# The spectrum tasks of a convolution wait until the last block of powers has been issued

## The chip, the cores and the metric

The kernel runs on one core of a Trainium2 chip. The metric is the device time of one execution in microseconds (us), taken as the median over several runs.

## The reference

The output puts two independent layers side by side, each for a sequence of 2048 rows and a width of 448.

```python
# A: a state-space convolution
dt = exp(log_dt);  A = -exp(log_A_real) + 1j*A_imag;  C = (C_real + 1j*C_imag)*dt[:, None]
P = exp((A*dt[:, None])[:, :, None] * pos)          # 448 channels x 256 states x 2048 positions
K = 2*einsum("dn,dnl->dl", C, P).real                # one filter of 2048 taps for each channel
y = irfft(rfft(u_t, 2*L) * rfft(K, 2*L))[:, :, :L]   # causal convolution
a = y.T + u*D_skip
# B: softmax attention, 16 heads of 28
q, k, v = split(x @ wqkv);  p = softmax(q @ k.T * 28**-0.5);  b = (p @ v) @ wo
out = concatenate([a, b], -1)
```

## The kernel before

An opening stage projects queries, keys and values and prepares seeds of the powers for A. Everything after it is one long loop, and this case lies in the loop. The attention is cut into 16 units (4 groups of 4 heads, 4 chunks of 512 queries), and each unit into 16 tiles of 128 keys. The loop runs over `NS` = 256 steps `s`, with `u, kt = divmod(s, 16)`: step 192 begins unit 12. In each step TensorE multiplies four score tiles (`s0` to `s3`, written to `pss`), ScalarE takes their exponentials (`p`), and TensorE multiplies those of the step before with the values (`pv`, written to `po`). Up to step 236 each step also takes row maxima for a unit further ahead (`m0` to `m3`, scores in `pm`, reduced on VectorE to `mx`); the steps from 237 on are called `late` and have none.

The work of layer A is laid into the gaps. The order inside a step is written out by hand, and from here on every engine executes its instructions in the order in which they are issued:

```python
ORDER = ('m0', 's0', 'm1', 's1', 'v', 'f', 'pv', 'f', 'v', 'k', 'm2', 's2', 'm3', 's3', 'v')
```

- `k`: the filters. There are `NB` = 56 blocks. `k_begin(s)` starts block b in step 3.5 b or later, once the lists of the block before are empty. It fills `powers["e"]` with 9 GpSimd operations (three doublings; the last one has tiles of 128x1024) and `powers["g"]` with 9 parts on VectorE. Each `k` issues 3 of the first list and each `v` one of the second. Three products of the block follow as tasks 4, 5 and 6 steps after its start: two read both sets of powers (`pm<-e,g`), the third is `pm<-w,ko`.
- `f`: a slot, `slot(s)`. Late steps have one more. A slot takes the first thing that is due: an urgent task, a projection of a finished unit (`p_due`), a product of a block (`m_due`), and otherwise a task that `f_slot` picks, first of kind "s", then of kind "f".
- Kind "s" are the spectra: 16 jobs (2 halves of the channels by 8), possible from step 192 on, loaded two steps (`FL`) ahead. One job is four tasks: `forth(0)`; `last`, which is `forth(1)` and the two joins; `back(0)`, at least `GAP` = 3 slots behind `last`; `back(1)`. A `forth` is 16 small matmuls (`pm<-yk,mw`) and two products with the input's spectrum on VectorE (`pr<-pm,ub`). A join is two complex sums on GpSimd (`p<-pr,pr`). A `back` is 16 matmuls (`pm<-p,mw`), a copy on ScalarE and a store `z<-y` on SyncE's queue.
- Kind "f" are 8 finishing jobs of four tasks `one(i)` (`pm<-zi,wb`, then VectorE `ot<-pm,ut`). They read `z` back (`zi<-z`), three steps (`FL`) ahead; the first half of them needs 8 finished spectra, the second half all 16. `skip` multiplies their input on GpSimd (`ut<-ut,dsk`).

`fin(u)` ends a unit: in the second step after its end, `sums` and `scale` use VectorE (`rb`, `pm<-r`, `on`), and for the last four units four projections follow (`project`, 32 matmuls on `ua`). After the loop the remaining tasks are drained slot by slot.

Of the kernel before, what the change touches and what calls it, by code (L numbers as in the profile page):

```python
# [92 lines left out]
def body(ctx, tc, a, out):  # L93
# [5 lines left out]
    def pool(stack, name, bufs=1, space=None, side=None):  # L99
        kw = {} if space is None else {"space": space}  # L100
        if side:
            kw["side"] = side
        return stack.enter_context(tc.tile_pool(name=name, bufs=bufs, reuse_waits="tile", **kw))
# [807 lines left out]
    def job(j, p, uh_p, ps, b0=(2, 1, 1, 2, 2), b1=(2, 2)):  # L911
        kind, f, i = j
        return spectrum(f, i, p, uh_p, ps, b0) if kind == "s" else finish(f, i, p, ps, b1)
# [11 lines left out]
    powers = {"g": collections.deque(), "e": collections.deque()}  # L925
# [20 lines left out]
    k_due = collections.deque(range(NB))  # L946
# [14 lines left out]
    def f_load(s_, kind):  # L961

        if not f_jobs[kind] or f_loaded[kind]:
            return
        _, f, i = f_jobs[kind][0]
        if kind == "f" and s_done[0] < (f + 1) * N1 // 4:
            return
        if (kind, f, i) == ("f", 0, 0):
            if f_ready["s", 1] == NS:
                return  # L970
            f_p["f", 0] = f_p["f", 1] = pool(f1_st, "ff_p")
        if (kind, f) not in f_p or f_ready.get((kind, f), 0) > s_ + 2:
            return
        load, tasks, ahead = job(f_jobs[kind].popleft(), f_p[kind, f], kq_p, w_tile)
        load()
        if ahead:
            f_ahead.append((s_ + FL[kind] - 1, ahead))
        f_loaded[kind].append((max(f_ready.get((kind, f), 0), s_ + FL[kind]), tasks))

    def f_slot(s_, kind):  # L980
        f_load(s_, kind)
        while f_ahead and f_ahead[0][0] <= s_:
            f_ahead.popleft()[1]()
        if not f_tasks[kind]:
            if not f_loaded[kind] or f_loaded[kind][0][0] > s_:
                return False
            f_tasks[kind].extend(f_loaded[kind].popleft()[1])
            f_load(s_, kind)
        gap, t = f_tasks[kind][0]
        if n_slot[0] < f_next[kind] + gap:  # L990
            return False
        f_tasks[kind].popleft()
        t()
        s_done[0] += kind == "s" and not f_tasks[kind]
        f_next[kind] = n_slot[0]
        f_load(s_, kind)
        return True
# [10 lines left out]
    def slot(s_):  # L1008
        n_slot[0] += 1
        while free and free[0][0] <= n_slot[0]:  # L1010
            free.popleft()[1]()
        if urgent and urgent[0][0] <= n_slot[0]:
            urgent.popleft()[2]()
        elif s_ >= NS and f_slot(s_, "s"):
            pass
        elif p_due and p_due[0][0] <= s_:
            p_due.popleft()[1]()
        elif m_due and m_due[0][0] <= s_:
            m_due.popleft()[1]()
        elif u_due and u_due[0][0] <= s_:  # L1020
            u_part(*u_due.popleft()[1:])
        else:
            f_slot(s_, "s") or f_slot(s_, "f")
# [158 lines left out]
```

## Time and profile before

| | |
|---|---|
| runs | 1278.78, 1279.68 and 1281.36 us, median 1279.68 us |
| profiled execution | 1280.71 us, its span 1278.9 us |
| busy in the span: TensorE, VectorE, ScalarE, GpSimd | 94%, 74%, 75%, 66% |
| mean granted TensorE clock | 0.982 |

Times in the trace are us from the start of the span. A row of the timeline has the start, the duration, the engine, the line of the code, the operation, the written tile, an arrow, the read tiles, the shape and how many instructions the row merges; in brackets stands how long the engine had been idle and what ended that. All instructions are issued by one helper, so that all rows have its line, and tiles are told apart by their names. A row of the table by stretches has the stretch, its length, the busy time of TensorE, its weight loads, VectorE, ScalarE and GpSimd (with instruction counts), the granted TensorE clock, the share of the DMA engines and GB/s. A step is found in the trace by its first maximum matmul, `pm<-kdif,qhat`.

### The profile page before, as it was taken

The numbers are of one execution on the slowest core, as the hardware profiler recorded it, in microseconds if no ns is written. First come the engines' busy times: TensorE is split into PE (matmuls) and PEld (weight loads), VectorE is DVE, ScalarE is ACT, GpSimd is POOL, SyncE is SP. The second block draws the span as 40 slices with busy tenths as digits, with TensorE's granted clock in tenths as the row PEclk, the third lists the DMA queues.
The fourth block names the chain that finished last, engine by engine and source line by source line (L and its number), as shares of the span: only waits on it lengthen the run. The fifth ranks groups of instructions, "written<-read, shape, count | busy, mean of one in ns | idle before, by whom it ended". The sixth has DMA issues, their size and how long they took to land.

```text
span 1278.9 us, 31211 instructions
## 1 busy us (share of the span) xinstructions
PE 1199.8 (94%) x11569; PEld 669.9 (52%) x11569; DVE 942.6 (74%) x2138; ACT 959.2 (75%) x2146; POOL 843.5 (66%) x728
## 2 busy tenths in 40 slices
PE   6778887999999999999999999999997999999998
PEld 4667664555555555555555555555553545545333
DVE  5788966878777878887789889888996665646312
ACT  5888865788888888888888888888885766756553
POOL 2666740897788888778599999889984222424321
PEclk8999899899999999999999999999998999999999
DMA  6678789437554545365533133422314443647666
GB/s 195 215 254 297 268 287 358 120 88 195 155 147 115 164 118 178 110 228 178 170 88 104 49 88 103 148 82 71 99 43 141 157 161 135 210 151 236 201 179 164
DMA packets 203377, 206.08 MB, mean 161 GB/s; under 512 B 98201, under 2 KB 162265, under 8 KB 201177
## 3 DMA queue, kind: packets, MB, share of 16 engines
q1 hardware_dynamic: 202696, 203.50, 51.6%
q8 instruction: 91, 1.49, 0.5%
q10 hardware_dynamic: 528, 0.59, 0.2%
q14 instruction: 62, 0.50, 0.1%
HBM read 121.59 MB, written 82.18 MB: 159 GB/s over the span
## 4 chain that ended last, share of the span: by engine, by line
PE 72%; DVE 13%; POOL 5%; ACT 4%; issue 3%; DMA 2%; ACTq 0%; SPq 0%; POOLq 0%; DVEq 0%
PE pm L77 40%; PE pss L77 15%; PE po L77 15%; DVE mx L77 2%; DVE tri L77 2%; ACT rl L77 1%; ACT p L77 1%; DVE rl L77 1%; POOL qhat L77 1%; DVE g L77 1%; DVE zg L77 1%; POOL p L77 1%; DMA xn<-in_B_x 1%; POOL e L77 1%; PE pt L77 1%
## 5 line engine op out<-in xcount | busy, mean ns | idle before, releaser
L77 ACT ACTIVATE p<-pss 128x512 f32<-128x512 f32 x1024 | 561.9, 610 | 127.6 <-PE pss L77 124.3
L77 PE MATMUL pss<-qhat,khat 128*128 128x512 f32 x1024 | 402.0, 399 | 2.0 <-ACT p L77 2.0
L77 DVE TENSOR_REDUCE mx<-pm 128x1 f32<-128x512 f32 x480 | 308.2, 683 | 102.1 <-PE pm L77 100.5
L77 PE MATMUL pm<-khat,qhat 128*128 128x512 f32 x749 | 327.0, 440 | 14.3 <-DVE mx L77 5.4
L77 POOL TENSOR_TENSOR e<-e,sdb 128x256 f32<-128x256 f32 x168 | 201.9, 1202 | 110.8 <-ACT e L77 101.6
L77 PE MATMUL po<-p,v 128*32 128x512 f32 x2048 | 269.6, 595 | 0.0
L77 PEld LDWEIGHTS pm<-khat,qhat 128*128 128x128 f32 x749 | 140.9, 188 | 231.1 <-ACT p L77 53.7
L77 POOL TENSOR_TENSOR e<-e,eu 128x256 f32<-128x256 f32 x168 | 248.2, 1477 | 13.2
L77 DVE CUSTOM_DVE_ANT_0 rl<-pm,rl 128x512 f32<-128x512 f32 x259 | 178.1, 688 | 68.1 <-ACT rl L77 65.8
L77 PEld LDWEIGHTS pss<-qhat,khat 128*128 128x128 f32 x1024 | 190.4, 188 | 45.5 <-issue 11.4
L77 POOL TENSOR_TENSOR eu<-e,sdb 128x256 f32<-128x256 f32 x168 | 202.0, 1202 | 0.0
L77 POOL TENSOR_TENSOR p<-pr,pr 64x448 f32<-64x448 f32 x64 | 73.1, 1142 | 149.1 <-PE pm L77 108.1
L77 ACT ACTIVATE rl<-pm 128x512 f32<-128x512 f32 x259 | 156.7, 606 | 15.6 <-PE pm L77 9.4
L77 DVE TENSOR_TENSOR g<-g,zg 128x128 f32<-128x128 f32 x392 | 162.0, 413 | 3.5
L77 PE MATMUL pm<-kdif,qhat 128*128 128x512 f32 x249 | 100.0, 402 | 6.7 <-DVE xn L77 4.3
L77 PE MATMUL pm<-xh,khat 128*128 128x512 f32 x256 | 84.4, 422 | 11.9 <-DVE hl L77 5.1
L77 DVE TENSOR_TENSOR zg<-g,zg 128x128 f32<-128x128 f32 x224 | 87.9, 393 | 5.0
L77 PE MATMUL pm<-e,g 128*32 128x64 f32 x3584 | 73.7, 223 | 10.7 <-POOL e L77 8.2
L77 PEld LDWEIGHTS pm<-e,g 128*32 128x32 f32 x3584 | 56.0, 110 | 49.1 <-POOL e L77 12.5
L77 DVE TENSOR_TENSOR pr<-pm,ub 128x448 f32<-128x448 f32 x64 | 36.8, 618 | 45.8 <-PE pm L77 30.3
L77 ACT ACTIVATE y<-pm 128x448 f32<-128x448 f32 x48 | 26.6, 555 | 58.4 <-PE pm L77 32.8
L77 ACT ACTIVATE ub<-pm 128x224 f32<-128x224 f32 (+1 forms) x96 | 38.6, 448 | 40.0 <-PE pm L77 38.1
(132 smaller groups left out, 1406.1 us busy)
## 6 DMA issues: line engine op xcount, KB each, us to landing
sdb<-sd SPq DMA_DIRECT2D x55, 336.0 KB
qhat<-q SPq DMA_DIRECT2D x64, 256.0 KB
khat<-k SPq DMA_DIRECT2D x64, 256.0 KB
sd<-sg SPq DMA_DIRECT2D x8, 1456.0 KB
k<-hl SPq DMA_DIRECT2D x16, 512.0 KB
mw<-in_mw SPq DMA_DIRECT2D x16, 512.0 KB
sd<-qhat SPq DMA_DIRECT2D x8, 896.0 KB
yu_d<-ub SPq DMA_DIRECT2D x64, 112.0 KB
```

The lines of the kernel that those rows point to most:

```text
L77: i = f(*args, **kw)
```

## The change

`f_slot` still loads the next job, but takes up no task, and runs no `skip`, while a block of powers is still to begin or a list of powers still holds something. Nothing else differs.

```diff
     def f_slot(s_, kind):
         f_load(s_, kind)
+        if k_due or powers["e"] or powers["g"]:
+            return False
         while f_ahead and f_ahead[0][0] <= s_:
             f_ahead.popleft()[1]()
```

## The prediction

> **What bounds the kernel now.** I began with the page: TensorE is busy 94% of the span and carries most of the chain that ended last, so the question is where TensorE stands still.
>
> ```profile
> PE 1199.8 (94%) x11569; PEld 669.9 (52%) x11569; DVE 942.6 (74%) x2138; ACT 959.2 (75%) x2146; POOL 843.5 (66%) x728
> PE 72%; DVE 13%; POOL 5%; ACT 4%; issue 3%; DMA 2%; ACTq 0%; SPq 0%; POOLq 0%; DVEq 0%
> ```
>
> Next came TensorE's waits from 900 us to the end (who waited for what: total, times, longest). One wait stands out: 6.5 us in one piece for powers (`e`) from GpSimd.
>
> ```profile
> PE pm L77 <- POOL e L77: 6.5, 1, 6.5
> PE pm L77 <- POOL p L77: 2.1, 3, 0.8
> ```
>
> The timelines of GpSimd and TensorE show how it comes about.
>
> ```profile
> 950.88 1.91 POOL L77 TENSOR_TENSOR e<-e,sdb 128x1024 f32<-128x1024 f32 x1
> 962.12 1.31 POOL L77 TENSOR_TENSOR e<-e,eu 128x512 f32<-128x512 f32 x1
> 976.35 4.77 POOL L77 TENSOR_TENSOR p<-pr,pr 64x448 f32<-64x448 f32 x4 [12.93 <-DVE pr L77]
> 981.20 1.91 POOL L77 TENSOR_TENSOR e<-e,sdb 128x1024 f32<-128x1024 f32 x1
> 983.07 1.90 POOL L77 TENSOR_TENSOR eu<-e,sdb 128x1024 f32<-128x1024 f32 x1
> 985.05 2.32 POOL L77 TENSOR_TENSOR e<-e,eu 128x1024 f32<-128x1024 f32 x1
> ...
> 968.75 0.96 PE L77 MATMUL pm<-yk,mw 128*32 128x224 f32 x16 [0.37 <-DVE pm L77]
> 974.05 0.94 PE L77 MATMUL pm<-yk,mw 128*32 128x224 f32 x16
> 987.42 1.08 PE L77 MATMUL pm<-e,g 128*32 128x64 f32 x32 [6.46 <-POOL e L77]
> 989.98 1.63 PE L77 MATMUL pm<-p,mw 128*32 128x224 f32 x16
> ```
>
> GpSimd had finished two of the three doublings of a block at 963.43 (962.12 + 1.31). It then stood 12.93 us, because the next in its queue were four joins of the first spectrum, which need `pr` from VectorE and so the `forth` matmuls that TensorE reaches only at 968.75 and 974.05. The last doubling, three instructions that depend on nothing of this, came behind the joins and ended at 987.37 (985.05 + 2.32); TensorE had been waiting for it since 980.97 (987.42 - 6.46).
>
> This is block 55, the last one. It cannot begin before step 192.5, so it begins in 193; its first product comes four steps on, in 197, which makes the step of 987.42 step 197. The first `forth` is due two steps after the load in 192, in 194. The doublings are issued at the `k` of steps 193, 194 and 195, and `last` in the second slot of 195, which stands before that step's `k`. The order on GpSimd follows.
>
> Here are the steps around it, from one matmul `pm<-kdif,qhat` to the next (columns: stretch, length, busy times of PE, PEld, DVE, ACT, POOL, granted clock, DMA share, GB/s). They are steps 194 to 199, step 197 cut at the end of the wait.
>
> ```profile
> 965.44:971.23 5.79, 4.68 (x65) 2.37 (x64) 5.15 (x13) 3.23 (x8) 0.00 (x0) 1.00 1.04 380
> 971.23:976.36 5.13, 4.75 (x49) 2.39 (x49) 4.22 (x10) 3.29 (x7) 0.01 (x1) 1.00 0.93 305
> 976.36:979.87 3.51, 3.38 (x16) 1.58 (x17) 3.48 (x9) 2.34 (x5) 3.39 (x3) 1.00 0.05 7
> 979.87:987.42 7.55, 1.09 (x5) 0.56 (x4) 1.50 (x4) 2.36 (x5) 7.26 (x5) 0.81 0.00 0
> 987.42:992.58 5.16, 5.16 (x60) 2.70 (x61) 0.50 (x1) 0.97 (x3) 0.00 (x0) 0.61 0.00 0
> 992.58:996.84 4.26, 4.26 (x66) 2.55 (x65) 1.98 (x5) 3.22 (x8) 0.00 (x0) 1.00 0.17 58
> 996.84:1001.07 4.23, 4.23 (x50) 2.53 (x48) 2.33 (x6) 3.09 (x7) 0.00 (x0) 1.00 0.19 60
> ```
>
> Together they take 35.63 us (1001.07 - 965.44). Step 197 takes 12.71 (7.55 + 5.16), where step 198 with the same kinds of task, one product and one `back`, takes 4.26. The excess is 8.45: the wait of 6.46 and 1.99 more, because the granted clock behind the wait was 0.61. The Trainium skill (TensorE: Matmul & The Clock Gate, What's actually happening) says that an idle window of about 3.4 us halves the clock and that about as long a busy one restores it. That would be half of 3.4, 1.7 us by its figure, instead of my 1.99, and the gain forecast below would be 0.3 us smaller.
>
> **The change, part by part.** The gate opens when the last part of the last list is issued. Powers `e` are out at the `k` of step 195. Powers `g` go one at each `v`; the first falls to the `v` behind `k` in step 193, then three a step, so the ninth goes at the second `v` of step 196, behind both slots. In step 197 the first slot belongs to the product, the second is the first that can take `forth(0)`. So: `forth(0)` moves from 194 to 197, `last` from 195 to 198, `back(0)` and `back(1)` from 197 and 198 into the two slots of 200 (three slots behind `last`), and the second job's `forth(0)` from 199 to 201. Steps 194 to 199 hold five tasks of spectra before and two after.
>
> *GpSimd's queue.* Nothing now stands between the second and the last doubling. That one takes 6.13 to 6.2 us (981.20 to 987.37 above), hence ends near 969.6. TensorE asks for it in step 197. Steps 194 to 196 are rebuilt below at 5.2, 3.48 and 3.05, so step 197 starts at 977.2 and its product a little over 1 us later (980.97 - 979.87 = 1.10), at 978.3. The cover is 8.7 us, and both the wait and the slow clock go. The joins pass behind the powers: they start at the earliest when `last` has run in step 198, when GpSimd has nothing else.
>
> *The six steps.* Costs come from steps with the same content:
>
> ```profile
> 679.77:684.86 5.09, 4.03 (x49) 1.87 (x48) 5.06 (x12) 3.54 (x8) 4.93 (x4) 1.00 0.15 54
> 850.45:856.09 5.64, 4.12 (x49) 1.98 (x48) 5.50 (x15) 3.47 (x8) 5.48 (x3) 1.00 0.79 258
> 908.43:913.33 4.90, 3.99 (x34) 1.86 (x33) 4.87 (x12) 3.82 (x8) 4.67 (x6) 1.00 0.00 0
> 920.33:923.78 3.45, 3.45 (x33) 2.02 (x32) 3.13 (x8) 3.21 (x8) 3.29 (x4) 1.00 0.00 0
> 923.78:926.83 3.05, 3.05 (x18) 1.51 (x17) 2.84 (x8) 2.47 (x6) 2.89 (x3) 1.00 0.70 138
> ```
>
> The first three are steps in which a unit is scaled beside one product, which is what step 194 becomes; VectorE is full in them. The mean is 5.2. Step 195 keeps one product, 3.45; step 196 has nothing, 3.05. Steps 197 and 198 have a product and a `forth`, 4.26 as step 198 now; step 199 one product, 3.45. The sum is 5.2 + 3.45 + 3.05 + 4.26 + 4.26 + 3.45 = 23.7 us against 35.6: 11.9 us less.
>
> *What is given back.* Three tasks of spectra now lie behind step 200. Their price is TensorE's:
>
> ```profile
> 1030.04:1033.11 3.07, 3.07 (x18) 1.50 (x16) 2.60 (x6) 2.56 (x6) 2.50 (x3) 1.00 0.51 202
> 1033.11:1037.66 4.55, 4.55 (x49) 2.62 (x48) 2.00 (x5) 4.14 (x9) 2.08 (x2) 1.00 0.16 54
> 1069.13:1073.01 3.88, 3.88 (x34) 2.03 (x33) 3.78 (x8) 2.50 (x6) 0.43 (x1) 1.00 0.94 348
> ```
>
> A step with none takes 3.07, with one 3.88, with two 4.55: 0.81 for a single task, 0.74 each in a pair. Three cost 2.2 to 2.4; I take 2.4. The order of two tasks in a step and of empty steps changes between 200 and 247, which by these rows moves 0.07 a task and is inside that. The pattern of both tasks in one step, an empty step, both `back`s in the next (1030.04 and 1033.11 are its end) stands in the trace already without a wait for joins.
>
> *The late steps.* Counting both orders slot by slot, the lag is three tasks at step 200, one from about step 224 on. It puts `last` of the fifth job of the second half into step 238 instead of 237. Late steps are short, and three slots then no longer cover two joins:
>
> ```profile
> 1178.33 4.76 POOL L77 TENSOR_TENSOR p<-pr,pr 64x448 f32<-64x448 f32 x4 [0.77 <-PE pss L77]
> 1183.15 0.96 PE L77 MATMUL pm<-p,mw 128*32 128x224 f32 x16 [0.80 <-POOL p L77]
> 1191.06 0.96 PE L77 MATMUL pm<-p,mw 128*32 128x224 f32 x16 [0.56 <-POOL p L77]
> 1193.47 0.96 PE L77 MATMUL pm<-p,mw 128*32 128x224 f32 x16 [0.78 <-POOL p L77]
> ```
>
> The fifth job waits 0.80 now, the sixth, wholly in late steps, 0.56 + 0.78 = 1.34. I give the fifth the sixth's wait and a little more for it, 0.7 us in all. The bounds are none and twice the 1.34, 2.7. The last two jobs have a projection between `last` and `back`.
>
> *SyncE's queue.* The loads of the first job stay in step 192; those of the second move from 194 to 197, to before a `forth` four steps later. The last `back` goes from step 245 to the first slot of 246, and the load of the first finishing job of the second half from the second slot of 246 to the third. The finishing jobs wait three steps for their loads, so from step 248 on both orders are the same; the drain after the loop is not touched, and I cost it at nothing, covered by that wait.
>
> The sum: 11.9 - 2.4 - 0.7 = 8.8 us. From the profiled execution that is 1280.71 - 8.8 = 1271.9; it lies 1.0 above the median of the runs, so for the median 1279.68 - 8.8 = **1270.9 us**.
>
> **The rivals.**
>
> *One step late at the end.* If `z` is not back in time or the load slips one slot, all finishing jobs of the second half come a step later.
>
> ```profile
> 1245.64:1255.00 9.36, 8.80 (x70) 3.39 (x69) 1.56 (x4) 6.30 (x14) 1.34 (x2) 1.00 1.08 311
> 1229.05 0.48 SPq L77 DMA_DIRECT2D zi<-z  x1
> 1236.29 0.58 PE L77 MATMUL pm<-zi,wb 128*32 128x224 f32 x8
> ```
>
> Three such steps take 9.36, one 3.1: 1274.0 us. For it: the margin in the order is one slot. Against it: from the issue of `zi` to its first reader there are 7.2 us now.
>
> *Slower.* The same mechanism with more steps: the finishing jobs come one per three steps, so if the gate opened so late that the lag were four steps at their first load, 12.5 us would be lost at the end: 1279.7 + 3.7 = 1283.4. It decides from three steps on (9.4 against 8.8). That needs block 55 to begin three or more steps later than 193; against it stands its first product four steps behind step 193 in the order above.
>
> *VectorE holds up GpSimd.* The last doubling moves beside a VectorE that is busy 5.15 of 5.79 and 4.22 of 5.13 us. If GpSimd got only the rest, 1.55 us, it would be short by 4.6 at 976.36 and end at 981, TensorE would wait nearly 3 us, and the clock with it: about 1275. Against it: the same instruction took 1.91 us at 950.88, in ordinary steps like that of 923.78 (VectorE busy 2.84 of 3.05), and 1.91 at 981.20, when VectorE was nearly idle. The Trainium skill (SBUF — State Buffer, Who interferes with whom) describes an exclusive lock between the two for VectorE operations with two SBUF inputs or in a two-port mode; these equal durations show no such lock here.
>
> *The change does not act,* or the wait moves to the joins in step 200: then 11.9 shrinks by 8.45 or more and the result is within 0.2% of before, 1277 to 1281. Against it: the two `forth`s that GpSimd stood for are themselves moved.
>
> **How the numbers follow.** 0.2% or 2.6 us is about what a measurement of this kernel can tell from no change. The forecast has 0.66, one step late 0.14, held-up powers 0.03, a partial gain from dearer joins 0.05, no change 0.06, slower 0.06. The first four are all faster, 0.88; same 0.06; slower 0.06. For the range: step 194 at 4.90, tasks at 0.74 and no late wait give 12.2 - 2.2 = 10.0, 1269.7; like steps differ by up to 0.7 (4.90 and 5.64), and one or two of the six better by as much make the low end 1268.5. At the high end step 194 at 5.64 and late waits of 2.7 give 11.5 - 2.4 - 2.7 = 6.4, 1273.3, and one step late 1274.0; with a little of both, 1275.5.
>
> **What would show it.** In the trace after: the three 128x1024 operations of block 55 directly behind its 128x512 ones; no wait of TensorE for `e` near step 197 and a granted clock of 1.00 there; steps 194 to 199 in about 24 us; the first joins behind the last powers; waits for `p` in late steps of about 2.8 instead of 2.1 us in total; the last nine steps unchanged. The prediction is wrong if `pm<-e,g` or the first `pm<-p,mw` still waits several us, if steps 200 to 247 grow by more than 5 us, or if the drain grows.

## The result, and the profile after

The changed kernel takes 1273.45 us (median of 4 runs, 1271.97 to 1275.26) against 1280.49 us before in the same comparison: ratio 0.9948, 95% interval 0.9936 to 0.9961, 7.0 us or 0.55% faster. Forecast were 1270.9 us, 8.8 below the median then known, and a range of 1268.5 to 1275.5, in which the result lies. The profiled execution took 1275.26 us, the longest of the four, with a span of 1273.5; the profile of a second run of the same kernel, `after_again` below, has a span of 1271.2.

GpSimd's timeline after:

```profile
962.56 1.31 POOL L77 TENSOR_TENSOR e<-e,eu 128x512 f32<-128x512 f32 x1
963.95 1.91 POOL L77 TENSOR_TENSOR e<-e,sdb 128x1024 f32<-128x1024 f32 x1
965.82 1.92 POOL L77 TENSOR_TENSOR eu<-e,sdb 128x1024 f32<-128x1024 f32 x1
967.81 2.36 POOL L77 TENSOR_TENSOR e<-e,eu 128x1024 f32<-128x1024 f32 x1
986.62 4.81 POOL L77 TENSOR_TENSOR p<-pr,pr 64x448 f32<-64x448 f32 x4 [16.45 <-DVE pr L77]
```

The last doubling of block 55 follows the second one directly and ends at 970.17. TensorE begins its product at 978.19, so 8.0 us of cover are left. The joins come 16 us later, when GpSimd has nothing else to do.

TensorE's waits from 900 us on:

```profile
PE pm L77 <- POOL p L77: 3.5, 3, 2.2
PE pss L77 <- ACT p L77: 1.7, 6, 0.3
PE pm L77 <- DVE on L77: 1.4, 3, 0.6
PE pm L77 <- DMA zi<-z: 0.9, 1, 0.9
```

The wait of 6.5 us for `e` is gone. In its place there is more waiting for joins (3.5 instead of 2.1 us) and a wait of 0.9 us for the first finishing job's read-back, which was not there before.

Steps 194 to 199 after, in the columns of the prediction:

```profile
965.89:970.47 4.58, 3.82 (x50) 1.95 (x49) 4.48 (x12) 3.07 (x7) 4.21 (x2) 1.00 1.00 376
970.47:973.95 3.48, 3.48 (x34) 1.94 (x32) 3.37 (x8) 2.81 (x6) 0.00 (x0) 1.00 0.37 141
973.95:976.99 3.04, 3.04 (x18) 1.58 (x17) 2.73 (x8) 2.55 (x6) 0.00 (x0) 1.00 0.78 180
976.99:981.82 4.83, 4.59 (x65) 2.45 (x64) 3.06 (x7) 3.07 (x8) 0.00 (x0) 1.00 0.57 216
981.82:986.62 4.80, 4.55 (x64) 2.39 (x65) 3.05 (x7) 2.79 (x7) 0.00 (x1) 1.00 0.00 0
986.62:990.24 3.62, 3.62 (x32) 2.02 (x33) 2.24 (x5) 2.79 (x6) 3.43 (x3) 1.00 0.02 5
```

They take 24.35 us (990.24 - 965.89), the clock is full throughout, and the tasks lie in the slots that the prediction counted. The rest of the run is cut at the matmuls with the values (`po<-p,v`) of step 236 and at the last group of them. The stretch between these two cuts is called the late steps from here on, what follows is the drain. First come the late steps and the drain of before, then those of the first profile after, and last two rows of the second profile, steps 194 to 199 and the late steps:

```profile
1172.36:1257.82 85.46, 81.30 (x805) 32.72 (x799) 21.45 (x48) 48.04 (x93) 28.72 (x21) 1.00 0.74 217
1257.82:1278.90 21.08, 15.84 (x180) 6.69 (x174) 4.64 (x10) 3.39 (x7) 2.09 (x1) 0.98 0.35 97
```

```profile
1162.47:1252.38 89.91, 83.79 (x821) 33.70 (x815) 21.59 (x48) 49.15 (x94) 28.68 (x21) 0.98 0.74 217
1252.38:1273.50 21.12, 15.84 (x180) 6.69 (x174) 4.64 (x10) 3.40 (x7) 2.10 (x1) 0.96 0.37 100
```

```profile
964.97:989.31 24.34, 23.15 (x257) 12.33 (x256) 18.89 (x42) 17.08 (x36) 7.64 (x5) 1.00 0.46 159
1161.54:1250.12 88.58, 82.30 (x821) 33.16 (x815) 21.57 (x48) 49.11 (x94) 28.64 (x21) 1.00 0.74 221
```

| us against before | first profile | second profile |
|---|---|---|
| up to step 194, where nothing differs | +0.45 | -0.47 |
| steps 194 to 199 | -11.28 | -11.29 |
| step 200 to the `pv` of 236 | +0.94 | +0.94 |
| from there to the loop's end | +4.45 | +3.12 |
| drain | +0.04 | 0.0 |
| span | -5.4 | -7.7 |

So 11.3 us are saved in six steps and 4.1 to 5.4 are given back, about four fifths of it after step 236.

### The profile page after: what moved, and what is told of

The parts are those of the page before. It is cut to its first block, busy times and chain, and to the rows that moved or that the text cites. A ratio compares the mean times of both kernels' runs of the same rounds, so it can differ in the third digit from the quotient of the medians.

```text
span 1273.5 us, 31219 instructions
## 1 busy us (share of the span) xinstructions
PE 1199.4 (94%) x11569; PEld 670.1 (53%) x11569; DVE 943.5 (74%) x2138; ACT 959.4 (75%) x2146; POOL 844.4 (66%) x728
## 4 chain that ended last, share of the span: by engine, by line
PE 71%; DVE 14%; ACT 5%; POOL 4%; issue 4%; DMA 1%; ACTq 0%; SPq 0%; DVEq 0%; POOLq 0%
PE pm L77 40%; PE pss L77 15%; PE po L77 15%; DVE mx L77 2%; DVE tri L77 2%; ACT rl L77 2%; ACT p L77 2%; DVE rl L77 1%; DVE g L77 1%; POOL qhat L77 1%; DVE zg L77 1%; ACT tri L77 1%; DVE sg L77 1%; DVE hl L77 1%; DVE px L77 1%
```

## The experiments

Each kernel was compared with the kernel before in the same series: median 1280.78 us for the first four, 1280.20 for the last four.

**after_again**: the changed kernel unaltered.

> The changed kernel once more, as the yardstick beside the next three. Theory (the wait of 6.46 us and the slow clock behind it go; steps 194 to 199 take 24.4 instead of 35.6 us; about 4.5 us are given back in the late steps): 6 to 8 us faster than before, about 1273 us. If the profile of the first run had a chance delay in its late steps (2.16 us for p, 0.91 us for zi), these waits are absent here and it comes nearer to 1270.9.

Measured: 1273.01 us (ratio 0.9940, 0.9928 to 0.9953). The waits for `p` are again 3.5 us in total, 1.6 the longest, and that for `zi` 1.0. They are no chance delay. The totals are equal, and TensorE is busy 1.5 us longer in the late steps of the first profile with the same instructions (83.79 against 82.30). So the 1.3 us between the two are the slow clock behind the longest wait, which only the first has.

**order_only**: only the order in GpSimd's queue.

```diff
         f_tasks[kind].popleft()
+        while kind == "s" and len(f_tasks[kind]) == 2 and powers["e"]:
+            powers["e"].popleft()()
         t()
```

> The gate is left out; only the order in GpSimd's queue is changed: what is left of the powers e is issued just ahead of the first joins. No task moves to another slot. Theory (order of GpSimd's queue): the wait for e and the slow clock go, steps 194 to 196 stay crowded, nothing lags and the late steps stay as before: 8.4 us faster, about 1272 us. Rival (the gain of the change comes from thinning out steps 194 to 196, where VectorE is full): at most 3 us faster, about 1277.5 us or more, and TensorE waits elsewhere in steps 196 to 198.

Measured: 1272.10 us (0.9931, 0.9918 to 0.9943), 8.7 us faster than before. The two stretches in its trace, steps 194 to 199 and the late steps:

```profile
963.31:990.21 26.90, 25.52 (x305) 13.98 (x304) 19.15 (x43) 18.39 (x38) 8.78 (x6) 1.00 0.47 162
1161.49:1246.94 85.45, 81.28 (x806) 32.72 (x800) 21.54 (x48) 48.16 (x93) 28.68 (x21) 1.00 0.74 219
```

On GpSimd the last doubling now ends before the joins, which still stand and wait for `pr`:

```profile
965.22 2.37 POOL L77 TENSOR_TENSOR e<-e,eu 128x1024 f32<-128x1024 f32 x1
973.97 4.81 POOL L77 TENSOR_TENSOR p<-pr,pr 64x448 f32<-64x448 f32 x4 [6.38 <-DVE pr L77]
```

With all its tasks in the slots of before, six steps shrink from 35.63 to 26.90 us, by 8.73, and the late steps stay at 85.45. GpSimd's order alone makes the whole of the wait and of the clock, and thinning out steps 194 to 196 is not needed for it: that rival falls.

**gate_last**: only the task with the joins waits, and only for the powers `e`.

```diff
         gap, t = f_tasks[kind][0]
+        if kind == "s" and len(f_tasks[kind]) == 3 and (k_due or powers["e"]):
+            return False
```

> Only the task with the joins waits, and only for the powers e: forth(0) stays in step 194, last moves from step 195 to the first slot of 196, and from step 197 on the order is that of before. Theory: steps 194 to 199 take 5.8 + 3.5 + 3.9 to 4.6 + 4.3 + 4.3 + 4.2 = 26.0 to 26.7 instead of 35.6 us, nothing is given back: 8.9 to 9.6 us faster, about 1271.3 us, 2 us faster than the whole change. Rival (the lag costs nothing, the late waits are chance): equal to the whole change within 0.7 us.

Measured: 1271.66 us (0.9929, 0.9916 to 0.9941).

```profile
964.04:990.74 26.70, 25.33 (x305) 14.16 (x304) 19.26 (x43) 18.19 (x38) 8.74 (x6) 1.00 0.47 163
1162.09:1247.53 85.44, 81.27 (x805) 32.72 (x799) 21.45 (x48) 48.05 (x93) 28.71 (x21) 1.00 0.74 217
```

Six steps take 26.70 us, the late steps 85.44 as before: nothing is given back. It comes out 1.4 us below the whole change in the medians; the intervals overlap, so that the times alone don't settle the difference, but in the traces the late steps are shorter by 3.1 us (88.58 - 85.44), and from step 194 to the end of the span it takes 304.6 us against 306.2. Its six steps are only 0.2 us better than those of `order_only`, though the second `forth` has left step 195.

**skip_with_first_task**: the whole change, `skip` issued later.

```diff
-            f_ahead.append((s_ + FL[kind] - 1, ahead))
+            tasks[0] = (0, lambda f=tasks[0][1]: (ahead(), f()))
```

> The whole change, and the GpSimd multiplication that prepares a finishing job (skip) is issued with the job's first task instead of a step earlier, so that it no longer stands ahead of the joins of step 238. Theory (part of what is given back is that joins wait behind a skip that itself waits for its transfer): TensorE's wait of 2.16 us for p in step 239 falls to about 0.7, with less of a slow clock behind it: 1.5 to 2.7 us faster than the whole change, about 1271.3 us. Rival (the joins are late because VectorE is): no difference.

Measured: 1279.27 us (0.9988, 0.9979 to 0.9997), 6 us slower than the whole change. The expectation failed, though the mechanism shows. First the changed kernel's GpSimd rows around step 238, then this kernel's of steps 235 and 236, then its waits of TensorE:

```profile
1171.32 2.11 POOL L77 TENSOR_TENSOR ut<-ut,dsk 128x896 f32<-128x896 f32 x1 [9.26 <-DVE pr L77]
1173.38 4.74 POOL L77 TENSOR_TENSOR p<-pr,pr 64x448 f32<-64x448 f32 x4
```

```profile
1158.44 4.75 POOL L77 TENSOR_TENSOR p<-pr,pr 64x448 f32<-64x448 f32 x4 [8.15 <-PE pm L77]
1163.28 2.07 POOL L77 TENSOR_TENSOR ut<-ut,dsk 128x896 f32<-128x896 f32 x1
```

```profile
PE pm L77 <- DVE ot L77: 5.1, 3, 3.4
PE pm L77 <- POOL p L77: 2.6, 4, 0.7
```

In the changed kernel a `skip` of 2.11 us stands directly ahead of the joins; without it there, the longest wait for `p` falls to 0.7 and the total to 2.6 us. But the `skip` of the finishing job before, now issued with that job's first task, stands behind the joins of step 235, `ot` waits for the `skip`, and TensorE waits for `ot`: 5.1 us, 3.37 in one piece. Behind that piece the granted clock is low, 0.59 from 1165.83 to 1170.00 us, which adds to the loss. It is the fault of the kernel before over again, with another pair of operations.

**late_joins_on_vector**: the whole change; late joins on VectorE. In the code `late[0]` holds from step 238 on; step 237 has no maxima either, but is not `late` and has no third slot.

```diff
-            nc.gpsimd.tensor_tensor(t_["p", e][:64], t_[0, 0][es], t_[1, 1][es], ALU.subtract)
-            nc.gpsimd.tensor_tensor(t_["p", e][64:], t_[0, 1][es], t_[1, 0][es], ALU.add)
+            eng = nc.vector if late[0] else nc.gpsimd
+            eng.tensor_tensor(t_["p", e][:64], t_[0, 0][es], t_[1, 1][es], ALU.subtract)
+            eng.tensor_tensor(t_["p", e][64:], t_[0, 1][es], t_[1, 0][es], ALU.add)
```

> The whole change, with the joins of steps 238 and later on VectorE, which has no maxima to take there. Theory (most of what is given back late is waits for joins on GpSimd, which the lag of one task lengthens): TensorE's 3.5 us of waits for p in late steps shrink to under 0.7 us; 2.5 to 4 us faster than the whole change, 1269 to 1270.5 us; the wait of 0.9 us for zi stays. Rival (the joins only fill time that TensorE would lose to other waits): within 1 us of the whole change.

Measured: 1271.11 us (0.9930, 0.9918 to 0.9941). Its late steps, and two of TensorE's waits from 900 us on:

```profile
1161.79:1247.57 85.78, 82.08 (x822) 33.54 (x816) 33.38 (x64) 48.90 (x94) 10.51 (x5) 1.00 0.78 229
```

```profile
PE pss L77 <- ACT p L77: 2.4, 7, 0.7
PE pm L77 <- DMA zi<-z: 1.2, 1, 1.2
```

No wait for joins is left among TensorE's waits, and the late steps fall from 88.58 to 85.78 us, by 2.8 as expected. The medians differ by 1.9 us, but the kernel before was 0.6 faster in this series too; the intervals overlap, and the 1269 to 1270.5 us expected were missed. The 2.8 us are not what the change had given back: moving these joins also removes waits that the kernel before had. The next run tells the two apart.

**gate_last_late_joins_on_vector**: both edits.

> The kernel in which only the task with the joins waits for the powers e, with the joins of steps 238 and later on VectorE. Theory: its 2.1 us of waits for p go and nothing else changes: 1.5 to 2.5 us faster than without, about 1269.5 us, and level with or below the whole change with late joins on VectorE. Rival (the lag of the whole change costs nothing once the joins are off GpSimd): both equal within 0.5 us.

Measured: 1270.08 us (0.9918, 0.9905 to 0.9931), the fastest here: 10.1 us or 0.8% below the kernel before. Its late steps:

```profile
1164.07:1247.90 83.83, 81.02 (x806) 32.89 (x800) 28.90 (x60) 48.04 (x93) 15.06 (x9) 1.00 0.76 222
```

They are 1.6 us shorter than without the second edit (85.44), while the whole change gained 2.8 by it. The difference, 1.2 us, is what the joins had to do with the 3.1 given back there. The other 1.9 to 2.0 stay (85.78 - 83.83): the wait for `zi`, 1.2 us in that run and absent here, and the third task. So the rival, that the lag costs nothing once the joins are off GpSimd, does not fit the traces; in the times the two kernels are 1.0 us apart, with overlapping intervals.

**lag_more**: the gate opens three steps later.

```diff
-        if k_due or powers["e"] or powers["g"]:
+        if NS - 64 <= s_ < 200 or k_due or powers["e"] or powers["g"]:
```

> The gate of the whole change stays shut up to step 199 and opens in 200, three steps later; by my count of the slots the finishing jobs of the second half then come two steps later. Prediction's rule (3.1 us for each step that they come late): 6.2 us, and about 1 us more of late waits: 1280 us, no faster than the kernel before. Rival (work is only moved and TensorE is the bound, so a lag costs little): within 1.5 us of the whole change, about 1273 to 1274.5 us.

Measured: 1272.67 us (0.9938, 0.9926 to 0.9950), level with the whole change. My rule fell, the rival was right. The rows are steps 194 to 199, step 200 to the `pv` of 237, from there to the loop's end, and the drain. The middle cut lies one step later than in the rows above, so that its 85.26 is not to be held against their late steps:

```profile
964.69:986.41 21.72, 21.00 (x225) 11.49 (x224) 16.76 (x38) 16.86 (x36) 4.20 (x2) 1.00 0.32 112
986.41:1162.22 175.81, 175.23 (x1622) 90.86 (x1624) 105.92 (x215) 112.37 (x221) 54.62 (x46) 1.00 0.52 173
1162.22:1247.48 85.26, 79.81 (x808) 31.65 (x800) 20.71 (x45) 45.99 (x89) 31.14 (x24) 1.00 0.71 214
1247.48:1270.90 23.42, 17.37 (x201) 7.58 (x200) 5.30 (x12) 3.79 (x7) 4.21 (x2) 0.97 0.58 158
```

Emptying the six steps saves another 2.6 us, and the drain grows by 2.3 (23.42 against 21.08): finishing tasks have moved into it, and it holds 201 of TensorE's matmuls instead of 180. The loop does not wait for late finishing jobs, it ends without them.

**pad_8**: the whole change with more GpSimd work ahead of the doubling's end.

```diff
+            for _ in range(9 if b == NB - 1 and i == 2 else 1):
-            nc.gpsimd.tensor_tensor(uts[0], t[:, ::-1, :, :m], zi, ALU.mult)
+                nc.gpsimd.tensor_tensor(uts[0], t[:, ::-1, :, :m], zi, ALU.mult)
```

> The whole change, with the 128x1024 multiplication into eu in the last doubling of block 55 repeated 8 times, to the same result: 15.3 us more in GpSimd's queue ahead of the doubling's end. In the changed kernel that end lies at 970.2 and TensorE asks at 978.2, so the cover is 8.0 us. Theory: a wait of about 7.3 us for e in step 197 and some 2 us of slow clock behind it: 9 us slower than the whole change, about 1282 us, the loss of the kernel before made anew by GpSimd alone. Rival (the gain came from thinning out steps 194 to 196 and from the moved loads): under 4 us slower.

Measured: 1283.30 us (1.0022, 1.0012 to 1.0031). The wait is back, and step 197 as a whole:

```profile
PE pm L77 <- POOL e L77: 7.8, 1, 7.8
```

```profile
976.52:990.87 14.35, 6.26 (x66) 2.98 (x64) 3.07 (x7) 3.20 (x8) 8.72 (x5) 0.76 0.19 74
```

Step 197 takes 14.35 instead of 4.83 us: 7.82 of waiting and 1.7 for the clock. Nothing but GpSimd's queue was altered: together with `order_only` this shows the cause from both sides.

## Why the prediction was right, and where it was off

**The wait and its clock: right.** 8.45 us were to go; moving GpSimd's order alone takes 8.73 out of the six steps, and putting work back ahead of the doubling brings the loss back. The cover was forecast at 8.7 us and is 8.0.

**The six steps: 11.9 forecast, 11.3 measured, by two errors that partly cancel.** Step 194 cost 4.58 where I took 5.2 from steps with a scaling. Steps 197 and 198 cost 4.83 and 4.80 where I took 4.26. That price was mis-sized: the step I read it from held a `back`, copied once by ScalarE; a `forth` keeps its `pm` tile for two products on VectorE, and the next maximum matmul that wants the tile waits (VectorE's and TensorE's timelines after). This wait is 0.24 us of the 0.57 by which step 197 is dearer; the rest was not traced to one cause.

```profile
980.52 1.16 DVE L77 TENSOR_TENSOR pr<-pm,ub 128x448 f32<-128x448 f32 x2 [1.43 <-PE pm L77]
```

```profile
981.82 0.47 PE L77 MATMUL pm<-kdif,qhat 128*128 128x512 f32 x1 [0.24 <-DVE pr L77]
```

So the two `forth` tasks did not become cheaper by leaving the crowded steps: 24.35 us and three tasks at 0.8 make 26.75, as much as the 26.70 and 26.90 of the two kernels that leave `forth(0)` where it was.

**Three tasks at 2.4 us: too dear.** Two of them, up to step 236, cost 0.94 together, where 0.74 to 0.81 each was forecast; the third lies in the late steps. With 0.8 for that one the three make 1.7. TensorE is busy 1.3 us longer in that stretch (172.12 against 170.80) and stands still 0.4 less; why was not tested.

**The late steps: 0.7 us forecast, the step that failed.** They grew by 3.1 and 4.5 us, where 0.7 and the third task's 0.8 were forecast. Beside that task (0.8 is an estimate), TensorE waits 1.4 us more for joins and 0.9 to 1.0 for `zi`, and in one of the two profiles the clock halves behind the longest wait. I had priced the fifth job like the sixth and left out the `skip` ahead of its joins, although the row of before (a start of joins 0.77 us after a `skip`) was at hand. Without that `skip` the fifth job waits 0.69 and 0.60 us in `skip_with_first_task`, like the sixth.

**Read-back of `z`: costed at nothing, wrongly.** I read 7.2 us from the issue of `zi` to its first reader as margin. After, the issue is at 1223.75 and the reader at 1230.85, released by the transfer (SyncE's queue and TensorE's timeline):

```profile
1223.75 0.47 SPq L77 DMA_DIRECT2D zi<-z  x1
```

```profile
1230.85 0.59 PE L77 MATMUL pm<-zi,wb 128*32 128x224 f32 x8 [0.91 <-DMA zi<-z]
```

So the 7.1 us were the time until the transfer landed, and no margin. With the load one slot later it no longer fits; the three kernels that load in the slot of before (`order_only` and the two with `gate_last`) show no such wait. A kernel that changes only this slot was not tried. The forecast that the last nine steps stay unchanged is wrong by this wait. The rival built on it, one step late at 3.1 us, did not happen: the order held. Its price was wrong as well, as `lag_more` shows, where the finishing jobs come two steps later and no 6 us are lost; the slower rival stood on the same price.

**VectorE beside GpSimd: right to discount.** The three operations took 1.91, 1.92 and 2.36 us from 963.95 on, the last two of them beside step 194, in which VectorE was busy 4.48 of 4.58 us, against 1.91, 1.90 and 2.32 next to an idle one.

By the second profile the sum is 11.3 - 0.9 - 3.1 = 7.3 us. The late steps were 1.6 dearer than forecast and the six steps saved 0.6 less, while the two tasks before step 236 were some 0.7 cheaper: that these partly cancel is luck. Single executions vary besides: step 194 begins between 963.31 and 966.26 us in these profiles, with the same instructions ahead of it.

## What to carry to other kernels

On an engine that works strictly in order, look at what stands behind an instruction that waits: here four joins held up 6 us of work that was ready, and letting the ready work pass was worth 0.7%. Reorder only what has to pass (the joins) and leave the tasks in their slots; holding whole tasks back moves the same kind of wait to a place where the steps are shorter (in the traces here that cost 1.6 us; the times alone do not settle it). A stretch from issue to first use is margin only if the transfer is shown to end earlier.

## What was not expected of the hardware

Behind a wait of 2.16 us in step 239 the clock halved. Three stretches of half a microsecond from the first profile after:

```profile
1175.00:1175.50 0.50, 0.00 (x0) 0.00 (x0) 0.00 (x0) 0.00 (x0) 0.50 (x1) 1.00 0.97 288
1177.00:1177.50 0.50, 0.50 (x6) 0.00 (x0) 0.00 (x0) 0.44 (x1) 0.50 (x1) 0.50 0.07 24
1180.00:1180.50 0.50, 0.50 (x6) 0.26 (x2) 0.00 (x0) 0.41 (x1) 0.00 (x0) 1.00 0.00 0
```

The clock is 0.50 from about 1176.3 to 1179.7 us. In `after_again` a wait of 1.65 us at the same place left it at 1.00, and so did one of 1.92 us in `pad_8`. These are three single waits, and no threshold follows from them. The Trainium skill (TensorE: Matmul & The Clock Gate, What's actually happening) names an idle window of about 3.4 us as what halves the clock and a busy one of that length as what restores it; the restoring agrees with the 3.4 us here, the halving came after a shorter idle time.
